# A spectral mixing kernel: the first chunk's input summed in PSUM, one row by cosines alone, and channel products spread one to a slot

## The chip, the cores and the metric

The kernel runs on one core of a Trainium2 chip. The metric is the device time of one execution in microseconds (us). The kernel before took 505.17 us, the median of three runs (504.72 to 506.06).

## The reference

For x of shape (8, 3136, 256), so 8 batches of 3136 rows:

```
X  = real part of fft(fft(x, axis=1), axis=2)
h  = X^T U V                       # U: 3136x32, V: 32x3136, along the rows
u  = X + h^T
out = u + max(u @ w1, 0) @ w2      # w1: 256x1024, w2: 1024x256
```

Everything is float32 outside; the kernel computes its products in bf16 with float32 sums.

## The kernel before, in words

**The transform along the rows** is a product with tables of sines (`tabs[0]`) and cosines (`tabs[1]`, shown as tabc). Symmetry is used four times. The rows n and 3136-n are folded (`along_d`, L255, and `alone`, L265, fold along d; `mirror`, L278, and `half`, L282, along n), on VectorE from two float32 copies of a batch in SBUF (xf by an indirect DMA on GpSimd's queue, L53; xr by a DMA of SyncE's queue, L70; each has a fringe of one partition, loaded by `load_0`, L76 and L79). The folded batch is `G[b % 2][par]`, bf16: columns 0 to 127 go with the sines, 128 to 255 with the cosines, 256 and 257 belong to d = 128. The tables carry 32 further columns (393 to 424), the table times U, so that one product gives the transform and its projection on U; for d = 128 another 32 columns (425 to 456), written by `u_128` (L541). So a product is QW = 425 or TW = 457 columns wide.

**seq(b, par, typ, pn)** (L303) makes one product group: four or eight matmuls (L327) into a PSUM bank. typ 0 is the sine part, typ 1 the cosine part; par and pn are the parities of the output and of the fold. The group pn = 0 is copied out by ScalarE (`ev`, L335), and when pn = 1 is there VectorE adds and subtracts the two into the rows of `B` (typ 0, L351 and L355) or `A` (typ 1, L351 and L353), and the U part into `tab` (L339). In typ 0, pn = 0, four of the eight matmuls put d = 128 into row 0 of B.

**The transform along d** works on column groups of 392 (`chan`, L366, and `chan_odd`, L374): A times a cosine matrix, copied by ScalarE to `ca` (L372), B times a sine matrix, then VectorE writes S = ca + psb and T = ca - psb (L381, L382). `lowrank` (L385) makes `TA` from `tab` (copied by ScalarE, L394). What symmetry leaves apart is put into further rows of `VA`, whose first 32 rows are V: the odd half of one column by `apart_odd` (L410, a DMA and a ScalarE copy L416) and d = 128 by `apart_128` (L396, three ScalarE copies L402, L404, L406 and a DMA L408).

**front(c)** (L431) makes `u` for a chunk of 512 rows, channels on partitions: TA times VA in PSUM (`ph`, L437), then VectorE adds S or T (L445), then a transposing DMA of SyncE's queue gives `ut`. **first_product** (L451): 16 matmuls with W1 (L457) per chunk in eight slots, each slot's result through a Relu on ScalarE into `h` (L459). **second_product** (L461): 32 matmuls with W2 (L473) per chunk, VectorE adds `ut` (L479 to L482), a DMA stores the chunk. There are 49 chunks of eight slots.

**The order.** Up to slot 22 the program is in the order written (`manual_schedule`, closed at L663); behind it a scheduler moves the instructions of each engine. Each engine, and each DMA queue, takes its instructions in order. The steps of later batches are put into the slots by `spread` (L648): for batch b the fold (`fold`, L286) from slot end-49 to mid, the transform (`transform`, L492) from mid to end, where end is the slot in which front(c + 1) first needs batch b (slot 43 for batch 1) and mid = end-19 (end-21 for batch 1). Inside a transform `chan(ch)` and `chan_odd(ch)` follow each other.

Batch 0 has no earlier chunk beside it: tables, fold, products, lowrank, channel groups 0 and 1, then front(0) and the first W1 product come one after another. There the products of the sine part are begun (part 0) when half of G is there, and the group's cosine matmuls for d = 128 come later (part 1), when columns 128 to 257 are folded. PSUM has three banks with the tag "dft" (products, channel groups, ph), three with "p1" (W1's results, and three of the first products), two for W2's.

Of the kernel before, what the change touches and what calls it, by code (L numbers as in the profile page):

```python
# [28 lines left out]
def kernel(  # L29
# [101 lines left out]
    EOR_ = cpool.tile([KP, 2, NI, 258], BF16, name="eor")  # L131
    EOS = cpool.tile([KP, 2, NI, 258], BF16, name="eos")
    for t in (EOF_, EOR_):
        nc.vector.memset(t.rearrange("p a i d -> p (a i) d")[:, :, 0:1], 0.0)
        nc.vector.memset(t.rearrange("p a i d -> p (a i) d")[:, :, 256:258], 0.0)
    G = [[cpool.tile([KP, NI, GW], BF16, name=f"g{s}{par}", tag=f"g{s}{par}") for par in range(2)]
         for s in range(2)]
    for par in range(2):
# [123 lines left out]
            nc.vector.tensor_tensor(dst[:, a, :, 192:256], src[:, a, :, 1:128:2],  # L262
                                    src[:, a, :, 255:128:-2], op=AL.add)

    def alone(a, src, dst):  # L265
# [20 lines left out]
    def fold(b):  # L286

        nxt = b + 1 < B
        for a in range(2):
            for src, dst, load in ((xr, EOR_, load_r), (xf, EOF_, load_f)):  # L290
                yield lambda a=a, src=src, dst=dst: (alone(a, src, dst), along_d(a, src, dst, 0))
                yield lambda a=a, src=src, dst=dst: along_d(a, src, dst, 1)
                if nxt:
                    yield lambda a=a, load=load: load(b + 1, a)
            yield lambda a=a: mirror(a, slice(0, 128), AL.subtract)
            yield lambda a=a: mirror(a, slice(128, 258), AL.add)
        if nxt:
            yield lambda: load_0(x, xf, xr, b + 1, D)
        for par in range(2):
            yield lambda par=par: half(b, par, slice(0, 128))  # L300
            yield lambda par=par: half(b, par, slice(128, 258))

    def seq(b, par, typ, pn, part=None):  # L303
# [11 lines left out]
        if part == 1 or (part == 0 and ("pt", par, pn) in d):  # L315
            pt = d["pt", par, pn]
        elif part == 0 and (par, pn) != (0, 1):
            pt = psum.tile([P, TW], FP32, tag="p1", name="pt1", bufs=3)
        else:
            pt = psum.tile([P, TW], FP32, tag="dft", name="pt", bufs=3)  # L320
        mm = [(typ, 128 * typ, i) for i in ktiles(pn)]
        if typ == 0 and pn == 0:
            mm += [(1, 256, i) for i in ktiles(0)]
        for n, (t, col, i) in enumerate(mm):
            if part is None or (part == 1) == (col == 256):
                w = TW if typ == 0 and (pn == 1 or n == 0 or col == 256) else QW
                nc.tensor.matmul(pt[:, :w], g[:kp(i), i, col:col + P], tabs[t][:kp(i), i, par, :w],  # L327
                                 start=(n == 0), stop=(n == len(mm) - 1))
        w = QW if typ == 1 else TW
        if part == 0:  # L330
            d["pt", par, pn] = pt
            return
        if pn == 0:
            ev = d["ev", par] = wp.tile([P, TW], FP32, tag="ev", name="ev", bufs=2)
            nc.scalar.copy(ev[:, :w], pt[:, :w])  # L335
# [4 lines left out]
        if typ == 0:  # L340
# [24 lines left out]
    def chan(b, ch):  # L365

        d = ST[b]
        lo, hi = columns(ch)
        pt = d["pst"] = psum.tile([P, NQ], FP32, tag="dft", name="pst", bufs=3)
        nc.tensor.matmul(pt[:, :hi - lo], MC1[:], d["A"][:, lo:hi], start=True, stop=True)  # L370
        ca = d["ca"] = wp.tile([P, NQ], FP32, tag="ca", name="ca", bufs=2)
        nc.scalar.copy(ca[:, :hi - lo], pt[:, :hi - lo])  # L372

    def chan_odd(b, ch):  # L374

        d = ST[b]
        lo, hi = columns(ch)
        pt = psum.tile([P, NQ], FP32, tag="dft", name="psb", bufs=3)
        nc.tensor.matmul(pt[:, :hi - lo], MS1[:], d["B"][:, lo:hi], start=True, stop=True)  # L379
        ca = d["ca"]  # L380
        nc.vector.tensor_tensor(d["S"][:, lo:hi], ca[:, :hi - lo], pt[:, :hi - lo], op=AL.add)  # L381
        nc.vector.tensor_tensor(d["T"][:, lo:hi], ca[:, :hi - lo], pt[:, :hi - lo],  # L382
                                op=AL.subtract)
# [9 lines left out]
                n += 1  # L393
        nc.scalar.copy(TA[b % 2][:R, :], pt[:])  # L394

    def apart_128(b, part, lo=0, hi=HALF // 2 + 1):  # L396


        Q = HALF // 2
        row, v = VA[b % 2][R:R + 1], ST[b]["B"][0:1]  # L400
        if part == 0:
            nc.scalar.copy(row[:, lo:hi], v[:, Q - lo:(Q - hi if hi <= Q else None):-1])  # L402
# [89 lines left out]
    def transform(b):  # L492

        for par, typ in ((0, 1), (0, 0), (1, 1), (1, 0)):
            for pn in range(2):
                yield lambda par=par, typ=typ, pn=pn: seq(b, par, typ, pn)
        yield lambda: (lowrank(b), apart_odd(b, 0), apart_128(b, 3))
        yield lambda: apart_128(b, 0)
        yield lambda: apart_odd(b, 1)
        for ch in range(4):  # L500
            yield lambda ch=ch: chan(b, ch)
            yield lambda ch=ch: chan_odd(b, ch)
            if ch in (1, 2):
                yield lambda ch=ch: apart_128(b, ch)

    CK = {}
    ST = {}
# [24 lines left out]

    for part in range(2):
        along_d(0, xr, EOR_, part)
    alone(0, xr, EOR_)
    for part in range(2):
        along_d(1, xr, EOR_, part)
    alone(1, xr, EOR_)
    us, uc = list(transform_u(0)), list(transform_u(1))

    def u_128(pk):  # L541
# [15 lines left out]

    for a in range(2):
        along_d(a, xf, EOF_, 0)
        alone(a, xf, EOF_)  # L560
        mirror(a, slice(0, 128), AL.subtract)
    u_128(1)
    for par in (1, 0):
        half(0, par, slice(0, 128))

    nc.gpsimd.iota(pint[:], pattern=[[0, 1]], base=D, channel_multiplier=-1)
# [10 lines left out]
        load_r(1, a)  # L577
    halve(1)

    for par in (1, 0):  # L580
        for pn in range(2):
            seq(0, par, 0, pn, 0)
        if par == 1:
            uc[2]()
            uc[3]()
            u_128(0)
    for a in range(2):
        along_d(a, xf, EOF_, 1)
        mirror(a, slice(128, 258), AL.add)
# [51 lines left out]
    front(0)
    for ch in range(2, 4):
        chan(0, ch)
        chan_odd(0, ch)
# [58 lines left out]
```

## Time and profile before

| what | value |
|---|---|
| median of three runs | 505.17 us |
| the profiled execution | 506.69 us, span 504.9 us, mean granted clock 0.988 |
| TensorE busy | 466.4 us (92%), 3024 matmuls |
| VectorE busy | 340.3 us (67%) |
| ScalarE busy | 302.9 us (60%) |
| GpSimd busy | 57.6 us (11%) |
| DMA | 68.68 MB, mean 136 GB/s |
| W1, W2 matmuls (L457, L473) | 212.4 and 204.1 us |
| product groups (L327) | 78.3 us, 320 matmuls |
| TensorE busy in 0 to 30, 30 to 52, 52 to 60 us | 11.40, 16.96, 6.61 us |
| TensorE busy in 60 to 70, 70 to 80, 80 to 90 us | 9.27, 10.00, 7.25 us |
| VectorE busy in 60 to 70, 70 to 80, 80 to 90 us | 10.00, 8.27, 9.97 us |
| TensorE busy in 100 to 150, 200 to 250, 400 to 450 us | 49.16, 49.50, 47.97 us |

Times are from the start of the span. The views are: the chain that ended last (each piece was released by the one above it), the waits (who waited for whom, in total, times, longest), the timeline of an engine, and the busy time in stretches. In a timeline the first two numbers are start and duration, and the bracket is the idle time before the first instruction of the row with what released it. In a table of stretches the number behind the POOL column is the clock that was granted to TensorE.

### The profile page before, as it was taken

What the parts mean: (1) busy time and instruction counts of PE and PEld (TensorE: products, weight loads), DVE (VectorE), ACT (ScalarE), POOL (GpSimd) and SP (SyncE); (2) the same over time, 40 slices, a digit from 0 to 9 for tenths busy, and PEclk for the clock granted to TensorE, in tenths of its full rate; (3) what the DMA queues carried; (4) which work ended last, traced back from release to release, by engine and by line L of the source; (5) the groups of instructions that cost most, each with busy time, mean ns of one, the idle gap of its engine ahead of it and who ended that gap; (6) DMA issues with size and microseconds to landing.
All of it is one profiled execution on the core that took longest, in us unless ns stands there. A gap on an engine that the chain in (4) does not pass through costs nothing.

```text
span 504.9 us, 8167 instructions
## 1 busy us (share of the span) xinstructions
PE 466.4 (92%) x3024; PEld 294.6 (58%) x3024; DVE 340.3 (67%) x825; ACT 302.9 (60%) x541; POOL 57.6 (11%) x124
## 2 busy tenths in 40 slices
PE   0777797999999999999999999999999999899997
PEld 0643364556655666566656665566656665566665
DVE  8848998989799989999386246653545335444343
ACT  6915763575648654765567654955576555855662
POOL 6137034101122021120000000000000000000000
PEclk9999898999999999999999999999999999999999
DMA  6695497949977596585422533234233343333433
GB/s 185 172 197 138 109 227 162 233 116 235 214 203 205 161 265 182 134 209 136 108 69 75 126 83 80 64 105 126 64 78 84 106 124 55 86 84 106 125 84 125
DMA packets 84371, 68.68 MB, mean 136 GB/s; under 512 B 53854, under 2 KB 80292, under 8 KB 81180
## 3 DMA queue, kind: packets, MB, share of 16 engines
q1 hardware_dynamic: 80764, 53.41, 41.6%
q0 software_dynamic: 3568, 14.76, 10.7%
q8 instruction: 23, 0.38, 0.3%
q14 instruction: 16, 0.13, 0.1%
HBM read 29.26 MB, written 25.69 MB: 109 GB/s over the span
## 4 chain that ended last, share of the span: by engine, by line
PE 75%; ACT 9%; DVE 7%; DMA 5%; issue 2%; POOL 0%; SPq 0%; DVEq 0%; ACTq 0%; POOLq 0%
PE p L473 29%; PE p L457 28%; PE pt L327 10%; PE ph L437 4%; ACT h L459 3%; PE pu L223 2%; DMA uf<-in_moe_U_dram,xidx 2%; ACT va L416 1%; DMA xr<-in_x_dram 1%; DMA va<-A 1%; ACT ca L372 1%; ACT va L404 1%; PE psb L379 1%; DVE u L445 1%; ACT va L402 1%
## 5 line engine op out<-in xcount | busy, mean ns | idle before, releaser
L459 ACT ACTIVATE h<-p 128x512 bf16<-128x512 f32 x392 | 217.9, 597 | 127.1 <-PE p L457 126.5
L457 PE MATMUL p<-u,w 128*128 128x512 bf16 x784 | 212.4, 382 | 1.6 <-ACT h L459 1.6
L473 PE MATMUL p<-w,h 128*128 128x256 bf16 x1568 | 204.1, 273 | 0.4 <-ACT h L459 0.4
L473 PEld LDWEIGHTS <-h 128*128 128x128 bf16 x1568 | 153.5, 98 | 62.0 <-issue 2.6
L457 PEld LDWEIGHTS <-w 128*128 128x128 bf16 x784 | 76.3, 98 | 70.3 <-issue 13.8
L479 DVE TENSOR_TENSOR o<-p,ut 128x4 f32<-128x4 f32 (+1 forms) x100 | 16.0, 160 | 100.7 <-PE p L473 97.5
L327 PEld LDWEIGHTS <-g 98*128 98x128 bf16 x320 | 32.8, 104 | 41.7 <-issue 10.1
L327 PE MATMUL pt<-tabc,g 98*128 98x425 bf16 (+1 forms) x192 | 46.2, 377 | 6.0 <-DVE g L283 3.3
L335 ACT COPY ev<-pt 128x457 f32<-128x457 f32 (+1 forms) x32 | 16.9, 527 | 43.8 <-PE pt L327 41.3
L482 DVE TENSOR_TENSOR o<-p,ut 128x254 f32<-128x254 f32 (+1 forms) x100 | 40.5, 405 | 0.0
L481 DVE TENSOR_TENSOR o<-p,ut 128x254 f32<-128x254 f32 (+1 forms) x100 | 40.5, 405 | 0.0
L445 DVE TENSOR_TENSOR u<-ph,S 128x512 bf16<-128x512 f32 (+15 forms) x64 | 35.0, 556 | 1.0 <-PE ph L437 1.0
L327 PE MATMUL pt<-tabs,g 98*128 98x457 bf16 (+2 forms) x128 | 32.1, 380 | 3.5 <-DVE g L283 3.5
L437 PE MATMUL ph<-va,ta 128*128 128x512 bf16 (+18 forms) x128 | 31.6, 332 | 4.0 <-DVE T L382 1.9
L445 DVE TENSOR_TENSOR u<-ph,T 128x512 bf16<-128x512 f32 (+15 forms) x64 | 34.9, 555 | 0.0
L381 DVE TENSOR_TENSOR S<-ca,psb 128x392 bf16<-128x392 f32 (+1 forms) x32 | 18.0, 562 | 21.0 <-ACT ca L372 16.0
L53 POOL DMA_INDIRECT xf<-in_x_dram,xidx x16 | 19.2, 1203 | 110.6 <-DVE eof L262 68.8
L283 DVE TENSOR_TENSOR g<-eos 99x1024 bf16<-99x1024 bf16 (+1 forms) x32 | 21.4, 689 | 6.4 <-PE pt L327 6.4
L279 DVE TENSOR_TENSOR eos<-eof,eor 99x1024 bf16<-99x1024 bf16 (+1 forms) x32 | 21.0, 687 | 0.8 <-POOL eof L274 0.7
L257 DVE TENSOR_TENSOR eor<-xr 99x1016 bf16<-99x1016 f32 x16 | 19.3, 1208 | 1.5 <-DMA xr<-in_x_dram 1.5
L223 PE MATMUL pu<-gu,tabs 98*98 98x32 bf16 (+1 forms) x64 | 6.0, 251 | 15.1 <-DVE gu L194 15.1
L257 DVE TENSOR_TENSOR eof<-xf 99x1016 bf16<-99x1016 f32 x16 | 19.3, 1206 | 0.3 <-POOL eof L274 0.3
(113 smaller groups left out, 313.3 us busy)
## 6 DMA issues: line engine op xcount, KB each, us to landing
out_dram<-o SPq DMA_DIRECT2D x48, 512.0 KB
xr<-in_x_dram SPq DMA_DIRECT2D x16, 784.0 KB
va<-A SPq DMA_DIRECT2D x7, 196.1 KB
ut<-u SPq DMA_TRANSPOSE x49
w<-in_moe_w_ch_dram POOLq DMA_DIRECT2D x1, 512.0 KB, 10.6
out_dram<-o SPq DMA_DIRECT2D x4, 128.0 KB
va<-in_moe_V_dram POOLq DMA_DIRECT2D x2, 196.0 KB, 8.6
xf<-in_x_dram,xidx POOLq DMA_INDIRECT x16, 7.9
```

The source lines that it names most:

```text
L53: nc.gpsimd.indirect_dma_start(out_, None, bass.AP(t.tensor, t.offset, [[w, rows], [1, w]]), bass.IndirectOffsetOnAxis(idx, 0), element_of ...
L257: nc.vector.tensor_tensor(dst[:, a, :, 1:128], src[:, a, :, 1:128], src[:, a, :, 255:128:-1], op=AL.subtract)
L279: nc.vector.tensor_tensor(EOS[:, a, :, cols], EOF_[:, a, :, cols], EOR_[:, a, ::-1][:, :, cols], op=op)
L283: nc.vector.tensor_tensor(G[b % 2][par][:, :, cols], EOS[:, 0, :, cols], EOS[:, 1, :, cols], op=AL.add if par == 0 else AL.subtract)
L327: nc.tensor.matmul(pt[:, :w], g[:kp(i), i, col:col + P], tabs[t][:kp(i), i, par, :w], start=(n == 0), stop=(n == len(mm) - 1))
L437: nc.tensor.matmul(ph[:, col:col + hi - lo], TA[b % 2][:, s * P:(s + 1) * P], VA[b % 2][:, lo:hi], start=True, stop=True)
L445: nc.vector.tensor_tensor(u[:, s, col:col + hi - lo], ph[:, col:col + hi - lo], src, op=AL.add)
L457: nc.tensor.matmul(p1[:], W1[:, s, j * P:(j + 1) * P], k["u"][:, s, :], start=(s == 0), stop=(s == 1))
L459: nc.scalar.activation(k["h"][:, j, :], p1[:], AF.Relu)
L473: nc.tensor.matmul(p2[:, t % w, :], h[:, j, rs], W2[:, j, :], start=(j == 0), stop=(j == JT - 1))
L481: nc.vector.tensor_tensor(o[:, ts, 1:P], p2[:, :w, 1:P], ut[:, ts, 1:P], op=AL.add)
L482: nc.vector.tensor_tensor(o[:, ts, P + 1:D], p2[:, :w, P + 1:D], ut[:, tT, P - 1:0:-1], op=AL.add)
```

## The change

Three things, all written out in the program.

**Batch 0's d = 128.** `alone(0, ...)` puts columns 0 and 128 of x side by side with one GpSimd copy instead of a copy and a signed product, and `seq` takes the column that goes to row 0 of B through the cosine table for both parities: four matmuls more in the groups (typ 0, pn = 1), none wider than 425. So `u_128` is not needed before batch 0's products; it goes to slots 8 and 10. Row 0 of B holds the finished row, so VA gets it by one DMA and one ScalarE copy (slot 12) in place of four ScalarE copies, a DMA and a VectorE operation. Parity 0 is taken first.

**The first chunk.** A new `front_first` sums u in two PSUM banks: sine matrix times B, cosine matrix times A, TA times V's 32 rows; ScalarE copies one half to `u`, VectorE the other. The channel groups of batch 0 are no longer ahead of it: chan(0, 0) follows it, and the slots 0 to 3 take chan(0, ch + 1) and chan_odd(0, ch).

**Later batches.** In `transform`, chan_odd(ch - 1) follows chan(ch), the ScalarE copy of `apart_odd` comes behind chan(0) instead of ahead of it, and the 21 steps are spread from mid to end-3. The fold of batch 1 starts at slot 4 instead of 2.

```diff
+    def alone(b, a, src, dst):
+        if b == 0:
+            nc.gpsimd.tensor_copy(dst[:, a, :, 128:257:128], src[:, a, :, 0:129:128])
+            return
...
         mm = [(typ, 128 * typ, i) for i in ktiles(pn)]
-        if typ == 0 and pn == 0:
+        if typ == 0 and b == 0:
+            mm += [(1, 256, i) for i in ktiles(1 - pn)]
+        elif typ == 0 and pn == 0:
             mm += [(1, 256, i) for i in ktiles(0)]
+        tw = TW if typ == 0 and b > 0 else QW
...
+        if b == 0:
+            if part == 0:
+                nc.sync.dma_start(out=row[:, :HALF + 1], in_=v)
+            elif part == 2:
+                nc.scalar.copy(row[:, HALF + 1:], v[:, HALF - 1:0:-1])
...
-        yield lambda: apart_odd(b, 1)
         for ch in range(4):
             yield lambda ch=ch: chan(b, ch)
-            yield lambda ch=ch: chan_odd(b, ch)
-            if ch in (1, 2):
-                yield lambda ch=ch: apart_128(b, ch)
+            yield (lambda: apart_odd(b, 1)) if ch == 0 else (lambda ch=ch: chan_odd(b, ch - 1))
+            if ch > 1:
+                yield lambda ch=ch: apart_128(b, ch - 1)
+        yield lambda: chan_odd(b, 3)
...
-    u_128(1)
-    for par in (1, 0):
+    for par in range(2):
         half(0, par, slice(0, 128))
...
-            u_128(0)
...
-    apart_128(0, 3)
-    lowrank(0)
-    nc.scalar.copy(VA[0][P // 2:, :CH], ST[0]["A"][P // 2:, :CH])
-    apart_odd(0, 0, CH)
-    for ch in range(2):
-        chan(0, ch)
-        chan_odd(0, ch)
...
+    def front_first():
+        u = cp.tile([P, 2, CH], BF16, tag="u", name="u", bufs=2)
+        ph = [psum.tile([P, CH], FP32, tag="p1", name="ph1", bufs=3) for s in range(2)]
+        h = [slice(s * P, (s + 1) * P) for s in range(2)]
+        for s in range(2):
+            nc.tensor.matmul(ph[s][:], MSN[:, h[s]], ST[0]["B"][:, :CH], start=True, stop=False)
+        lowrank(0)
+        for s in range(2):
+            nc.tensor.matmul(ph[s][:], MC[:, h[s]], ST[0]["A"][:, :CH], start=False, stop=False)
+        for s in range(2):
+            nc.tensor.matmul(ph[s][:], TA[0][:R, h[s]], VA[0][:R, :CH], start=False, stop=True)
+        nc.scalar.copy(u[:, 0], ph[0][:])
+        nc.vector.tensor_copy(u[:, 1], ph[1][:])
+        ut = cp.tile([P, 2 * CH // P, P], BF16, tag="ut", name="ut", bufs=3)
+        nc.sync.dma_start_transpose(out=ut[:], in_=u.rearrange("p s r -> p (s r)"))
+        CK[0] = dict(u=u, ut=ut)
+    front_first()
+    apart_odd(0, 0)
+    chan(0, 0)
...
+    for ch in range(4):
+        due[ch] = [lambda ch=ch: chan_odd(0, ch)]
+        if ch < 3:
+            due[ch].insert(0, lambda ch=ch: chan(0, ch + 1))
+    spread([lambda: apart_odd(0, 1), lambda: u_128(0), lambda: u_128(1), lambda: apart_128(0, 2)],
+           6, 14)
...
-        spread(list(fold(b)), max(end - 49, 2), mid)
-        spread(steps, mid, end)
+        spread(list(fold(b)), max(end - 49, 4), mid)
+        spread(steps, mid, end - 3)
```

More of the change, by code (lines that the diff above doesn't have):

```diff
@@ L133 @@
     for t in (EOF_, EOR_):
-        nc.vector.memset(t.rearrange("p a i d -> p (a i) d")[:, :, 0:1], 0.0)
-        nc.vector.memset(t.rearrange("p a i d -> p (a i) d")[:, :, 256:258], 0.0)
+        nc.vector.memset(t.rearrange("p a i d -> p (a i) d")[:, :, 0:258:257], 0.0)
     G = [[cpool.tile([KP, NI, GW], BF16, name=f"g{s}{par}", tag=f"g{s}{par}") for par in range(2)]
@@ L263, in along_d @@
                                     src[:, a, :, 255:128:-2], op=AL.add)
-    def alone(a, src, dst):
+    def alone(b, a, src, dst):
+        if b == 0:
+            nc.gpsimd.tensor_copy(dst[:, a, :, 128:257:128], src[:, a, :, 0:129:128])
+            return
         nc.gpsimd.tensor_copy(dst[:, a, :, 128:129], src[:, a, :, 0:1])
@@ L290, in fold @@
             for src, dst, load in ((xr, EOR_, load_r), (xf, EOF_, load_f)):
-                yield lambda a=a, src=src, dst=dst: (alone(a, src, dst), along_d(a, src, dst, 0))
+                yield lambda a=a, src=src, dst=dst: (alone(b, a, src, dst), along_d(a, src, dst, 0))
                 yield lambda a=a, src=src, dst=dst: along_d(a, src, dst, 1)
@@ L314, in seq @@
         g = G[b % 2][par]
-        if part == 1 or (part == 0 and ("pt", par, pn) in d):
-            pt = d["pt", par, pn]
+        if part == 1:
+            pt = d.pop(("pt", par, pn))
         elif part == 0 and (par, pn) != (0, 1):
@@ L321, in seq @@
         mm = [(typ, 128 * typ, i) for i in ktiles(pn)]
-        if typ == 0 and pn == 0:
+        if typ == 0 and b == 0:
+            mm += [(1, 256, i) for i in ktiles(1 - pn)]
+        elif typ == 0 and pn == 0:
             mm += [(1, 256, i) for i in ktiles(0)]
+        tw = TW if typ == 0 and b > 0 else QW
         for n, (t, col, i) in enumerate(mm):
             if part is None or (part == 1) == (col == 256):
-                w = TW if typ == 0 and (pn == 1 or n == 0 or col == 256) else QW
+                w = tw if pn == 1 or n == 0 or col == 256 else QW
                 nc.tensor.matmul(pt[:, :w], g[:kp(i), i, col:col + P], tabs[t][:kp(i), i, par, :w],
                                  start=(n == 0), stop=(n == len(mm) - 1))
-        w = QW if typ == 1 else TW
         if part == 0:
@@ L334, in seq @@
             ev = d["ev", par] = wp.tile([P, TW], FP32, tag="ev", name="ev", bufs=2)
-            nc.scalar.copy(ev[:, :w], pt[:, :w])
+            nc.scalar.copy(ev[:, :tw], pt[:, :tw])
             return
@@ L339, in seq @@
         nc.vector.tensor_tensor(d["tab"][:, typ, par, :], pt[:, NQ:QW], ev[:, NQ:QW], op=AL.add)
-        if typ == 0:
+        if tw > QW:
             nc.vector.tensor_tensor(d["tab"][0:1, 0, par, :], pt[0:1, QW:TW], ev[0:1, QW:TW],
@@ L368, in chan @@
         lo, hi = columns(ch)
-        pt = d["pst"] = psum.tile([P, NQ], FP32, tag="dft", name="pst", bufs=3)
+        pt = psum.tile([P, NQ], FP32, tag="dft", name="pst", bufs=3)
         nc.tensor.matmul(pt[:, :hi - lo], MC1[:], d["A"][:, lo:hi], start=True, stop=True)
-        ca = d["ca"] = wp.tile([P, NQ], FP32, tag="ca", name="ca", bufs=2)
+        ca = d["ca", ch] = wp.tile([P, NQ], FP32, tag="ca", name="ca", bufs=2)
         nc.scalar.copy(ca[:, :hi - lo], pt[:, :hi - lo])
@@ L379, in chan_odd @@
         nc.tensor.matmul(pt[:, :hi - lo], MS1[:], d["B"][:, lo:hi], start=True, stop=True)
-        ca = d["ca"]
+        ca = d.pop(("ca", ch))
         nc.vector.tensor_tensor(d["S"][:, lo:hi], ca[:, :hi - lo], pt[:, :hi - lo], op=AL.add)
@@ L394, in lowrank, with apart_128 @@
         nc.scalar.copy(TA[b % 2][:R, :], pt[:])
-    def apart_128(b, part, lo=0, hi=HALF // 2 + 1):
+    def apart_128(b, part):
         Q = HALF // 2
         row, v = VA[b % 2][R:R + 1], ST[b]["B"][0:1]
-        if part == 0:
-            nc.scalar.copy(row[:, lo:hi], v[:, Q - lo:(Q - hi if hi <= Q else None):-1])
+        if b == 0:
[3 more added lines that the diff above has]
+                nc.scalar.copy(row[:, HALF + 1:], v[:, HALF - 1:0:-1])
+        elif part == 0:
+            nc.scalar.copy(row[:, :Q + 1], v[:, Q::-1])
         elif part == 1:
@@ L534 @@
         along_d(0, xr, EOR_, part)
-    alone(0, xr, EOR_)
+    alone(0, 0, xr, EOR_)
     for part in range(2):
         along_d(1, xr, EOR_, part)
-    alone(1, xr, EOR_)
+    alone(0, 1, xr, EOR_)
     us, uc = list(transform_u(0)), list(transform_u(1))
@@ L559 @@
         along_d(a, xf, EOF_, 0)
-        alone(a, xf, EOF_)
+        alone(0, a, xf, EOF_)
         mirror(a, slice(0, 128), AL.subtract)
-    u_128(1)
-    for par in (1, 0):
+    for par in range(2):
         half(0, par, slice(0, 128))
@@ L578 @@
     halve(1)
-    for par in (1, 0):
+    for par in range(2):
         for pn in range(2):
             seq(0, par, 0, pn, 0)
-        if par == 1:
+        if par == 0:
             uc[2]()
             uc[3]()
-            u_128(0)
     for a in range(2):
@@ L600 @@
         phase(pd[t][:], lrow.rearrange("p a l -> p (a l)"), pcol[:, t:t + 1], 17)
-    seq(0, 1, 0, 0, 1)
+    for pn in range(2):
+        seq(0, 0, 0, pn, 1)
     sine(MSN[:, 0:128], pd[0][:, 0:128], 17, -1)
     sine(MSN[:, 128:256], pd[0][:, 128:256], 17, 1)
-    seq(0, 0, 0, 0, 1)
+    seq(0, 1, 0, 0, 1)
     cosine(MC[:], pd[1][:], 17)
@@ L608 @@
     nc.scalar.copy(MC1[:], MC[:, :P])
+    seq(0, 1, 0, 1, 1)
     nc.gpsimd.tensor_copy(gate[0:1, 2:3], G[0][1][0:1, 0, 128:129])
@@ L624 @@
         nc.gpsimd.memset(G[1][par][:, :, 258:GW].bitcast(I32), 0)
-    for par in (1, 0):
-        seq(0, par, 0, 1, 1)
+    apart_128(0, 0)
     for par in range(2):
@@ L629 @@
             seq(0, par, 1, pn)
-            if (par, pn) == (0, 0):
-                apart_128(0, 0, 0, CH)
-    apart_128(0, 3)
-    lowrank(0)
-    nc.scalar.copy(VA[0][P // 2:, :CH], ST[0]["A"][P // 2:, :CH])
-    apart_odd(0, 0, CH)
-    for ch in range(2):
-        chan(0, ch)
-        chan_odd(0, ch)
     setup.close()
     cp = ctx.enter_context(tc.tile_pool(name="cp", bufs=2))
[L641 to L644, printed above, removed]
+    def front_first():
[17 more added lines that the diff above has]
+    chan(0, 0)
     due = {}
@@ L650, in spread @@
             due.setdefault(lo + (hi - lo) * n // len(steps), []).append(step)
-    spread([lambda: apart_128(0, 0, CH), lambda: apart_128(0, 1)], 1, 3)
-    spread([lambda: apart_odd(0, 1), lambda: apart_128(0, 2)], 7, 13)
+    for ch in range(4):
[4 more added lines that the diff above has]
+           6, 14)
     for b in range(1, B):
```

## The prediction

> **What bounds the kernel now.** I read the page first: TensorE is busy 92% of the span, so a change can win only where TensorE is idle or slow. The table of stretches says where: 11.4 of the first 30 us, 17.0 of the next 22, 7.25 of 10 at 80 to 90, and 49.2 of 50 from 100 on. So I read the chain of work that ended last, from 20 to 55 us:
>
> ```profile
> 26.38 0.29 DVE tabs L544
> 26.67 0.20 DVE tabc L544
> 26.87 0.61 DVE g L283
> 27.49 0.05 issue
> 27.54 3.15 PE pt L327 x8
> 30.69 2.87 PE pu L223 x32
> ...
> 34.02 0.29 DVE tabs L544
> 34.32 0.20 DVE tabc L544
> 34.52 0.59 DVE eof L260
> ...
> 38.41 1.32 DVE g L283 x2
> 39.74 0.05 issue
> 39.78 7.72 PE pt L327 x24
> 47.51 0.65 PE ptt L391 x4
> ```
>
> The reader is to see that `u_128` (L544) stands on the chain twice, and that the fold (L260 to L283) stands behind it only because VectorE takes its queue in order. The waits say what VectorE idled for in front of it:
>
> ```profile
> DVE tabs L544 <- ACT tabc L228: 5.6, 1, 5.6
> ...
> DVE tabs L544 <- ACT tabc L247: 1.7, 1, 1.7
> ```
>
> From the last product (47.50) to the first W1 matmul (53.29) there are 5.8 us of lowrank, channel groups and S, T, u with TensorE mostly waiting.
>
> The third place is batch 1. VectorE's timeline:
>
> ```profile
> 78.98 1.22 DVE L257 TENSOR_TENSOR eor<-xr 99x1016 bf16<-99x1016 f32 x1 [1.46 <-DMA xr<-in_x_dram]
> ```
>
> That is the fold of batch 2, placed by the scheduler ahead of batch 1's sums (L351, L353, done at 84.4), which free the bank that TensorE waits for (2.75 us, until 84.55). And the clock:
>
> ```profile
> 52.00:53.00 1.00, 0.70 (x3) 0.19 (x2) 1.00 (x3) 0.48 (x1) 0.00 (x0) 0.98 0.00 0
> 53.00:54.00 1.00, 1.00 (x4) 0.41 (x3) 1.00 (x3) 0.48 (x1) 0.00 (x0) 0.50 0.02 8
> 56.00:57.00 1.00, 0.71 (x3) 0.15 (x2) 1.00 (x2) 0.98 (x3) 0.00 (x0) 0.81 0.00 0
> ```
>
> The granted clock is half from 53.0 to 56.4, and again from 83.7 to 90.5. Ahead of 46.0 the column shows 1.00, but the matmuls themselves show otherwise: 425 columns go every 0.355 us, behind 46.0 every 0.18. So batch 0's products run at half clock until then. The changes of speed, 46.1, 53.0, 56.4, 83.7 and 90.5, lie on one grid of 3.41 us: full speed comes at a grid point after a step that was nearly all matmuls (87% busy was not enough at 42.7), half speed after one that was about half busy; 68% kept it.
>
> **The change part by part.**
>
> *Up to the fold.* GpSimd's products with signs go for batch 0, and with them two waits of 0.34 us (VectorE, L279); `u_128`'s wait of 1.7 us and its 0.5 us go. VectorE ends L279 at 23.96 (was 24.64), half of parity 0 at 24.6 (was 27.48), parity 1 at 25.2, L235 at 25.6. Then nothing holds it: two times 0.6 + 0.6 + 0.7, then g 2 x 0.65. The second half is there at 30.7 instead of 39.72, 9 us earlier. The batch 1 loads that follow (xf, GpSimd's queue) meet those of W1, V and W2, which are ahead of them in that queue and about 2 us earlier; they landed 7 to 11 us after issue, so by 37; needed at 42.
>
> *Products.* From 24.65: 8 of 425 columns at 0.355 (2.8), the 32 small ones as before (3.1), 8 more (2.8): 33.4. Then 16 for d = 128 (before 8: the change adds 8) and 16 of typ 1, with no gap. The small ones do not raise the clock (64 of them in 15.05 to 21.0 kept 0.093 us each), so the first full grid step after 30.55 ends between 34.0 and 37.4; on the old grid at 35.9. Until then 7 of the 32 at 0.355, the others at 0.18: 40.5 (39.4 to 41.1; 44.8 if it never came) against 47.50.
>
> The 8 added matmuls are 1.4 us of that. ScalarE's chain beside it (ev 0.5, sines 0.7, ev 0.5, 0.5, 0.5, two copies 0.5) ends at 39.0, GpSimd's row of signs in the sine matrix at 39.6, its W1 cast (1.03, which u's memory waits for) at 40.7: just hidden, and GpSimd's queue holds nothing else that is due.
>
> *First u.* B's matmuls 2 x 0.22 (41.05), lowrank's four 0.45 (tab is ready at 40.9), A's two behind VectorE's first sum (41.4): 42.0; TA's copy 0.36 lies under them, TA's two end at 42.45, and their result is read 0.17 later. A copy of 128x512 from PSUM on VectorE is not in the trace: L445's add of that size 0.68, L459 on ScalarE 0.60, bounds 0.5 and 0.7; I take 0.6, beside ScalarE's. First W1 matmul at 43.3 against 53.29: **10 us earlier**, 5.6 if the clock stayed at half.
>
> *What then is late.* All four channel groups now lie behind u. ScalarE is paced by ca 0.44 + h 0.52 a slot, VectorE by S and T, 0.94 a slot: they end at 48.1. The next u waits for the DMA of A into VA, which in SyncE's queue stands behind the transpose (1.3 us): issued at 45.2, with 2.74 to 4.27 us (the two rows of it on the chain, 367.72 and 422.80) landed at 47.9 to 49.4. I take the lower end, since the DMA engines moved nothing at 46 to 50 before. u of chunk 1 is done at 49.7 to 51.1, 6.4 to 7.8 us behind the first W1 (before 6.2). Copies L402 and L404 (1.3 us of ScalarE in that path) go. The B row's DMA (one partition; no row times its landing) has 9 us of cover, and the late copy of 1567 columns costs at most L416's 1.49 on ScalarE, which at 67 to 73 idles 0.6 to 1.1 us ahead of each pair of Relus.
>
> VectorE did batch 1's first L257 to L262 (2.33) in the gap ahead of that u; now they come behind it, with u_128's four (1.0). Before, u's end to the last g took 59.5 to 76.0, 16.5; now 19.8: 69.5 to 70.9, a gain of 5.1 to 6.5. So **of the 10 us about 4 are given back**: the first W1 is no longer what sets the end, VectorE's queue is. Batch 2's loads follow its folds, so the DMA that ended at 78.95 moves by about 5.3, and batch 1's first sums stand 1.34 us (L262 and the three of L479 to L482) further ahead in the new order: done at 84.4 - 5.3 - 1.34 = 77.8. TensorE goes on 6.7 us earlier than at 84.55.
>
> *Later batches.* From 100 on TensorE waits 2.0 us in all for `ca` ahead of psb, 1.6 for T ahead of ph, 1.1 for ca ahead of ph and pst. The first goes, since psb now comes a slot behind its ca. Bounds: all 4.7 gained, or lost in the rival below. I take 2.0.
>
> **Sum.** 504.9 - 6.7 - 2.0 = 496.2 of span. The profiled run took 506.69 and the median is 505.17; taken off the median: **496.5 us**.
>
> **The rivals.**
>
> *A: no half clock after batch 1's wait.* TensorE will again wait 2 to 3 us there; before, that cost 83.7 to 90.5 at half speed, of which 84.55 to 90.5 is 3.0 us of work. If the wait falls across a grid point, neither step is half idle and the 3.0 are saved, as far as VectorE (9.97 of 10 busy there) follows: 493.5 us. For it: 68% busy kept the clock at 59.8. Against: the wait is of the same size as before. [...]
>
> *B: the transfer is hidden anyway.* The DMA engines are full at 70 to 80 (share 1.01). If batch 2's xr still lands at 78.95, the sums come only the 1.34 earlier: 505.2 - 1.3 - 2.0 = 501.9. Against: the engines are near idle at 46 to 54, and the loads are issued by the folds.
>
> *C: the clock stays at half in batch 0.* First W1 at 47.7, slots of 1.5 us by TensorE (0.86 + 0.33 + 0.33), u of chunk 1 at 56.1, last g at 75.9: only the 1.3 stays, and 503.9 if later batches give nothing. It needs a gap in the products, such as a late g.
>
> *D: slower.* The eight groups of a transform go in 16 x 8/21 = 6 slots instead of 7, and the new order sets more of them side by side. A group's bank (three of "dft") is free only when VectorE has done three operations (0.17, 0.57, 0.59), and VectorE is 45.4 of 50 busy at 100 to 150 with folds up to 1.2 us long. Four waits of 1.2 in each of batches 1 to 3 are 14.4: 505.2 - 6.7 + 14.4 = 512.9. It decides from 0.7 us a wait. Against: the waits at that place are nil in the trace of batch 2 and later, and the new order keeps 1.3 us or more of other matmuls ahead of most.
>
> That the first u isn't summed as said is no rival: the changed kernel's instruction order shows the six matmuls and one add less on VectorE.
>
> **How the numbers follow.** Forecast 0.48, A 0.15, B 0.15, C 0.10, D 0.12. About 0.3% (1.5 us) is what a measurement of this kernel can tell from no change. Forecast, A and B are faster: 0.78; C is the same: 0.10; D slower: 0.12. The range leaves D out and reaches to C (504), and below A by half of the 4.7 us of waits: 491.5.
>
> **What would show it.** The second g at 31 (not 39.7); 425-column products every 0.18 us from about 36; first W1 at 43 to 44; chunk 1's u 6 to 8 us behind it; VectorE without idle time from there to the last g at 70; products of batch 1 waiting for g, which they did not before; TensorE's wait for A ending near 78; the waits for ca ahead of psb gone. It is wrong if VectorE's long stretch is not what batch 1 waits for (then up to 10 us stay), or if waits for A, B or g appear in batches 2 to 7.

## The result, and the profile after

The changed kernel took **498.63 us**, the median of four runs (497.33 to 500.51), against 505.13 us for the kernel before (504.72 to 506.06): a ratio of 0.987, 95% interval 0.984 to 0.991. It is faster, by 6.5 us (1.3%). The forecast was 496.5 us, in a range of 491.5 to 504.0.

The profiled execution took 498.67 us, span 496.9, against 506.69 and 504.9: 8.0 us less, where the sum had 8.7. VectorE is busy for 340.1 us, ScalarE for 299.4. TensorE's 461.2 us can't be held against the 466.4 before: 56 of its 3036 matmuls left no record in this profile. A second profile, which has them all, says 465.8.

This is the same view as the first one before, the chain of the work that ended last; columns are start, duration, what:

```profile
23.68 0.70 DVE g L285
24.39 0.05 issue
24.43 3.02 PE pt L332 x8
27.46 2.86 PE pu L222 x32
30.32 10.40 PE pt L332 x40
...
42.66 0.59 ACT u L653
43.26 0.04 issue
43.30 0.72 PE p L466 x2
...
45.06 3.21 DMA va<-A
48.27 0.14 issue
48.41 0.59 PE ph L446 x2
49.00 0.45 PE p L466 x2
49.44 0.67 DVE u L454
50.11 1.12 DVE eor L256
```

The reader is to see that `u_128` and the folds no longer stand among the products, that these go in one piece to 40.72, and that from the DMA of A into VA the chain goes to VectorE, and from u straight into batch 1's fold. Lines are shifted: products L332, W1 L466, front L446 and L454, folds L256 to L285, A L357.

The table of stretches has the clock behind the POOL column:

```profile
36.00:37.00 1.00, 1.00 (x5) 0.46 (x4) 0.90 (x3) 0.00 (x0) 0.00 (x0) 1.00 1.30 246
37.00:38.00 1.00, 1.00 (x7) 0.52 (x6) 0.35 (x2) 0.87 (x2) 0.00 (x0) 1.00 1.36 256
...
77.00:78.00 1.00, 0.36 (x2) 0.19 (x3) 1.00 (x5) 0.00 (x0) 0.00 (x0) 0.80 0.32 82
78.00:79.00 1.00, 1.00 (x4) 0.40 (x3) 1.00 (x3) 0.00 (x0) 0.00 (x0) 0.50 0.77 287
...
81.00:82.00 1.00, 1.00 (x8) 0.64 (x7) 0.97 (x5) 0.21 (x1) 0.00 (x0) 0.99 1.14 362
```

Four or five matmuls a us become seven at about 36.5, where the forecast had 35.9: batch 0's products did reach full clock. Behind batch 1's wait the clock is half for one step of 3.4 us (77.6 to 81.0); before it was two (83.7 to 90.5). That holds for this execution only: in the second profile of the changed kernel the matmuls go at half speed from the end of that wait, 78.64, to about 83.6 (four of 425 columns in 1.58 us, 0.9 at full speed), which is more than one step, and 12 W1 matmuls from 49.21 took 4.44 us where the first profile has 2.85. That wait, and VectorE's work ahead of it, in the timelines of TensorE and VectorE:

```profile
77.64 1.58 PE L332 MATMUL pt<-tabc,g 98*128 98x425 bf16 x4 [3.33 <-DVE A L357]
```

```profile
73.41 1.22 DVE L256 TENSOR_TENSOR eor<-xr 99x1016 bf16<-99x1016 f32 x1 [1.18 <-DMA xr<-in_x_dram]
...
76.92 0.58 DVE L357 TENSOR_TENSOR A<-ev,pt 128x392 bf16<-128x392 f32 x1
```

In TensorE's timeline before, the same wait was

```profile
84.55 1.58 PE L327 MATMUL pt<-tabc,g 98*128 98x425 bf16 x4 [2.75 <-DVE A L353]
```

The pattern is the old one, 6.9 us earlier: batch 2's fold waits for its DMA, batch 1's sums stand behind it, TensorE behind them. The DMA was issued at 65.39 and took 7.92 us; before, at 71.67 and 7.28.

From 100 us on TensorE's waits were 6.0 us in all, of these

```profile
PE psb L379 <- ACT ca L372: 2.0, 5, 0.5
PE ph L437 <- DVE T L382: 1.6, 4, 0.5
...
PE ph L437 <- ACT ca L372: 0.6, 2, 0.4
```

and are 3.6, of these

```profile
PE ph L446 <- ACT ca L376: 2.0, 4, 0.8
PE p L482 <- ACT h L468: 1.1, 2, 0.7
...
PE psb L383 <- ACT ca L376: 0.2, 1, 0.2
```

(us in total, times, longest). The 2.0 for `ca` ahead of psb is now 0.2 and the 1.6 for T is gone; the wait for `ca` ahead of ph rose from 0.6 to 2.0.

**Where the 10 us went** is read best from the starts of the transposes of ut, one a chunk, in the timeline of SyncE's queue, each less that of before (us). The rows below the first are the experiments, each one profiled execution.

| kernel | chunk 0 | 1 | 2 | 4 | 6 | 8 | 48 |
|---|---|---|---|---|---|---|---|
| after | -9.45 | -9.39 | -6.27 | -5.58 | -7.12 | -7.13 | -8.02 |
| after, again | -9.84 | -9.02 | -5.90 | -4.58 | -5.80 | -5.81 | -7.54 |
| old transform | -10.16 | -8.38 | -5.25 | -4.54 | -4.39 | -4.39 | -3.66 |
| new transform alone | 0.76 | 0.85 | 0.84 | -0.72 | -1.76 | -1.77 | -3.46 |
| groups first | -6.02 | -6.96 | -3.84 | -2.28 | -3.85 | -3.86 | -5.79 |
| fold in the gap | -7.40 | -7.58 | -6.76 | -8.69 | -9.56 | -9.57 | -11.10 |
| fold 2 behind | -10.42 | -10.22 | -7.10 | -13.67 | -13.51 | -7.68 | -11.30 |
| A's DMA ahead | -11.34 | -11.41 | -8.29 | -9.86 | -10.12 | -10.12 | -11.35 |
| these three | -8.38 | -8.77 | -7.95 | -14.53 | -14.37 | -9.20 | -11.62 |
| fold in two gaps | -10.61 | -11.00 | -9.07 | -8.42 | -10.00 | -10.01 | -12.17 |
| and u_128 on GpSimd | -10.02 | -10.41 | -8.88 | -8.46 | -7.74 | -7.74 | -9.94 |

In the changed kernel 3.1 us are lost from chunk 1 to chunk 2, on VectorE, another 0.7 by chunk 4, and 2.4 come back later. In its second profile, the same kernel stands up to 1.3 us from the first, so smaller differences between two rows say nothing.

### The profile page after: what moved, and what is told of

The parts are those of the page before. It is cut to its first block, busy times and chain, and to the rows that moved or that the text cites. A ratio compares the mean times of both kernels' runs of the same rounds, so it can differ in the third digit from the quotient of the medians.

```text
span 496.9 us, 8110 instructions
## 1 busy us (share of the span) xinstructions
PE 461.2 (93%) x2980; PEld 293.4 (59%) x3036; DVE 340.1 (68%) x819; ACT 299.4 (60%) x538; POOL 63.8 (13%) x120
## 4 chain that ended last, share of the span: by engine, by line
PE 66%; DVE 14%; DMA 8%; ACT 8%; issue 3%; POOL 0%; SPq 0%; DVEq 0%; ACTq 0%; POOLq 0%
PE p L482 26%; PE p L466 25%; PE pt L332 9%; PE ph L446 4%; ACT h L468 3%; DMA va<-A 3%; DMA out_dram<-o 2%; DVE eof L256 2%; DVE eor L256 2%; DMA uf<-in_moe_U_dram,xidx 2%; DMA xr<-in_x_dram 2%; ACT va L425 1%; DVE u L454 1%; ACT ca L376 1%; DVE eor L261 1%
## 5 line engine op out<-in xcount | busy, mean ns | idle before, releaser
L466 PE MATMUL p<-u,w 128*128 128x512 bf16 x729 | 202.7, 380 | 4.4 <-DVE u L454 1.5
L466 PEld LDWEIGHTS <-w 128*128 128x128 bf16 x784 | 75.9, 98 | 69.5 <-issue 9.2
L332 PEld LDWEIGHTS <-g 98*128 98x128 bf16 x328 | 32.9, 103 | 35.4 <-issue 7.0
L332 PE MATMUL pt<-tabc,g 98*128 98x425 bf16 (+1 forms) x200 | 44.9, 366 | 3.6 <-DVE A L357 3.3
L339 ACT COPY ev<-pt 128x425 f32<-128x425 f32 (+1 forms) x32 | 16.8, 526 | 40.2 <-PE pt L332 32.1
L490 DVE TENSOR_TENSOR o<-p,ut 128x254 f32<-128x254 f32 (+1 forms) x100 | 40.5, 405 | 0.0
L53 POOL DMA_INDIRECT xf<-in_x_dram,xidx x16 | 22.9, 1431 | 100.7 <-DVE eof L261 43.7
L454 DVE TENSOR_TENSOR u<-ph,S 128x512 bf16<-128x512 f32 (+23 forms) x63 | 34.2, 553 | 0.4 <-PE ph L446 0.4
L454 DVE TENSOR_TENSOR u<-ph,T 128x512 bf16<-128x512 f32 (+23 forms) x63 | 34.1, 552 | 0.0
L446 PE MATMUL ph<-va,ta 128*128 128x512 bf16 (+15 forms) x126 | 29.8, 328 | 4.4 <-ACT ca L376 2.0
L332 PE MATMUL pt<-tabs,g 98*128 98x457 bf16 (+2 forms) x128 | 31.8, 378 | 1.0 <-DVE g L285 0.9
L285 DVE TENSOR_TENSOR g<-eos 99x1024 bf16<-99x1024 bf16 (+1 forms) x32 | 21.3, 688 | 4.5 <-PE pt L332 4.4
L343 DVE TENSOR_TENSOR tab<-pt,ev 128x32 bf16<-128x32 f32 x32 | 6.0, 187 | 22.6 <-PE pt L332 22.2
L256 DVE TENSOR_TENSOR eof<-xf 99x1016 bf16<-99x1016 f32 x16 | 19.3, 1207 | 1.3 <-POOL eof L276 1.3
L256 DVE TENSOR_TENSOR eor<-xr 99x1016 bf16<-99x1016 f32 x16 | 19.3, 1206 | 1.2 <-DMA xr<-in_x_dram 1.2
```

Of the source, the lines that this page charges most:

```text
L53: nc.gpsimd.indirect_dma_start(out_, None, bass.AP(t.tensor, t.offset, [[w, rows], [1, w]]), bass.IndirectOffsetOnAxis(idx, 0), element_of ...
L256: nc.vector.tensor_tensor(dst[:, a, :, 1:128], src[:, a, :, 1:128], src[:, a, :, 255:128:-1], op=AL.subtract)
L285: nc.vector.tensor_tensor(G[b % 2][par][:, :, cols], EOS[:, 0, :, cols], EOS[:, 1, :, cols], op=AL.add if par == 0 else AL.subtract)
L446: nc.tensor.matmul(ph[:, col:col + hi - lo], TA[b % 2][:, s * P:(s + 1) * P], VA[b % 2][:, lo:hi], start=True, stop=True)
L454: nc.vector.tensor_tensor(u[:, s, col:col + hi - lo], ph[:, col:col + hi - lo], src, op=AL.add)
L466: nc.tensor.matmul(p1[:], W1[:, s, j * P:(j + 1) * P], k["u"][:, s, :], start=(s == 0), stop=(s == 1))
```

## The experiments

The theory: two parts make the gain, the front (VectorE's queue from the first u to the last g sets what is left of it) and the new transform of later batches. The rivals: the front alone, or a gain that is hidden behind batch 2's DMA. A diff is against the changed kernel unless said otherwise.

**The parts one by one.** These four ran beside each other; the kernel before took 505.18 us there (23 runs, 503.18 to 507.04).

Old transform, with the new front:

```diff
+        yield lambda: apart_odd(b, 1)
         for ch in range(4):
             yield lambda ch=ch: chan(b, ch)
-            yield (lambda: apart_odd(b, 1)) if ch == 0 else (lambda ch=ch: chan_odd(b, ch - 1))
...
+            yield lambda ch=ch: chan_odd(b, ch)
...
-        spread(steps, mid, end - 3)
+        spread(steps, mid, end)
```

> The changed kernel with the old transform: chan_odd(ch) right behind chan(ch), apart_odd's copy ahead of chan(0), steps spread to end. Theory: the sums of batch 1 stand 1.34 us later again on VectorE (L262 and the three additions to o ahead of them), and the waits for ca ahead of psb come back (1.7 us from chunk 4 to the last): 498.6 + 3.0 = 501.6 us, 0.993 of before. Rival (the later batches' part is worth nothing): 498.6 us, 0.987.

Measured: 503.01 us (12 runs, 499.41 to 506.64), ratio 0.995 (0.992 to 0.997). The median is 1.4 us above the theory's 501.6, which the interval (501.3 to 503.7 us) still holds; the rival's 498.6 lies outside. TensorE's waits for psb and for T from 100 us on are again those of before:

```profile
PE psb L383 <- ACT ca L376: 2.0, 5, 0.5
PE ph L446 <- DVE T L386: 1.9, 5, 0.5
```

New transform alone, on the kernel before:

```diff
-        spread(steps, mid, end)
+        spread(steps, mid, end - 3)
```

and the new order of its steps, as in the change.

> The kernel before with only the new transform (chan_odd a step later, apart_odd's copy behind chan(0), steps spread to end-3). Theory: the two gains of the part stand by themselves: 1.34 us at batch 1's wait for A (83.2 instead of 84.55) and 1.7 us later on: 502.1 us, 0.994 of before. Rival (denser transforms wait more for their PSUM banks, and the start hides it): 505 us or slower.

Measured: 502.57 us (6 runs, 501.18 to 504.4), ratio 0.994 (0.992 to 0.996), near the theory's 502.1 and against the rival. In TensorE's timeline the wait that was 2.75 us, until 84.55, is

```profile
82.51 0.89 PE L327 MATMUL pt<-tabc,g 98*128 98x425 bf16 x4 [0.29 <-DVE A L353]
```

and 1.8 us for A ahead of ph come behind it.

So each part is worth about half: 0.53% and 0.59%, together 1.1%, against 1.28% for the change. Whoever would have put the whole gain down to the first chunk, where 10 us are to be seen, would have missed half of it.

The changed kernel once more, as a control:

> The changed kernel again, beside the three others on the same chip: 498.6 us, 0.987 of before; wait for A ending at 77.6 us. If the start of its span differs from the first profile it will be in when TensorE's full speed comes in batch 0's products (34 to 37.4 us), since that grid is not tied to the program.

Measured: 499.23 us (6 runs, 496.03 to 502.37), ratio 0.988 (0.984 to 0.991). The time repeats, the places do not: batch 1's wait for A took 3.95 us and ended at 78.64, 1.0 later than in the first profile, although the first W1 matmul came 0.4 earlier, at 42.90.

Channel groups 0 and 1 ahead of the first u, as before the change, and the old front(0):

```diff
+    lowrank(0)
+    nc.scalar.copy(VA[0][P // 2:, :CH], ST[0]["A"][P // 2:, :CH])
+    apart_odd(0, 0, CH)
+    for ch in range(2):
+        chan(0, ch)
+        chan_odd(0, ch)
...
-    front_first()
-    apart_odd(0, 0)
-    chan(0, 0)
+    front(0)
```

> The changed kernel with channel groups 0 and 1, the copies into VA and the old front(0) put back ahead of the first W1 product; d = 128 by cosines alone and the new transform stay. Theory (VectorE's queue, from the first chunk's S and T to batch 1's first sums, sets the end of the start): the first W1 product starts 3 us later (40.6 + 5.8 = 46.4 against 43.3), chunk 1's u 2.5 us later, and all of that reaches the end, since VectorE has no idle time behind it: batch 1's wait for A ends near 80 (77.6 in the changed kernel) and the time is 501.1 us, 0.992 of before. Rival (the PSUM sum is hidden anyway, the gain came from the fold alone): 498.6 us and A at 77.6.

Measured: 502.11 us (10 runs, 498.12 to 505.42), ratio 0.993 (0.990 to 0.995). The number fits the theory (the wait for A ended at 80.94, where it had "near 80"), but its reason is mixed: the first W1 matmul came at 47.55 and not at 46.4. In TensorE's timeline:

```profile
44.97 1.01 PE L446 MATMUL ph<-va,ta 128*128 128x512 bf16 x2 [3.32 <-DMA va<-B]
```

The DMA of one row of B, 3.1 KB, was issued at 37.5 and landed 7.3 us later; in the changed kernel the DMA engines' share is 0.81 to 1.36 from 37 to 42 us. So this run does not price the order of the groups by itself; it shows what the cover that the prediction gave this DMA (9 us) is worth. It also has d = 128 by cosines and the new transform, and its ratio is 0.993 where the new transform alone has 0.994: what the new d = 128 is worth without the new first u can't be told from nothing.

**Where the 3 us behind chunk 1 go.** Four kernels ran beside each other, and two more later; the kernel before took 504.95 us there (10 runs) and 504.57 us (11 runs).

Batch 1's first fold (2.33 us) in VectorE's gap behind `phase`:

```diff
+    alone(1, 0, xr, EOR_)
+    for part in range(2):
+        along_d(0, xr, EOR_, part)
```

and it leaves `fold`.

> The changed kernel with the first piece of batch 1's fold (L256, L259, L261 and the GpSimd part, 2.33 us of VectorE) moved from behind chunk 1's u to the 2.6 us in which VectorE waits for batch 0's first product (33.5 to 36.1). No work changes. Theory (VectorE's queue from chunk 1's u on sets when batch 1's sums are done): the whole queue moves up by 2.3 us, batch 1's wait for A ends near 75.3 instead of 77.6 and the time is 496.6 us, 2.3 under the changed kernel. Rival (batch 2's fringe of xr, which takes 7.9 us to land with the DMA engines near full, is what VectorE waits for anyway): A at 77 or later, 498.9 us.

Measured: 496.38 us (4 runs, 495.83 to 499.11), ratio 0.985 (0.982 to 0.988). The time is the theory's; the way there is not. VectorE's timeline and TensorE's:

```profile
35.97 1.22 DVE L256 TENSOR_TENSOR eor<-xr 99x1016 bf16<-99x1016 f32 x1 [4.33 <-DMA xr<-in_x_dram]
```

```profile
39.52 2.52 PE L333 MATMUL pt<-tabc,g 98*128 98x425 bf16 x8 [2.13 <-DVE B L360]
```

The gap was not free: batch 1's data came only at 35.97, the fold held batch 0's sums up, the products waited 2.13 us for a bank, and the first W1 matmul came at 45.35, 2 us later than in the changed kernel. Still chunk 2 lost 0.8 instead of 3.1, and batch 1's wait for A fell from 3.33 to 0.7 us (with 1.8 for A ahead of ph behind it, where the changed kernel has 0.5). Late at the front, early where it counts.

Batch 2's fold behind batch 1's sums:

```diff
-            if 8 * c + j == 22:
+            if 8 * c + j == 44:
                 order.close()
```

> The changed kernel with the written order kept up to slot 44 instead of 22, so that batch 2's fold stands behind all of batch 1's sums on VectorE instead of ahead of the first. Theory: TensorE's wait for A (3.3 us) goes, and with it the stretch at half clock behind it (77.8 to 81.0, 1.6 us of work): 494 us. Rival (that fold is only put off: VectorE is busy 97 in 100 from 84 to 100, and batch 2's products then wait for g): what is gained at 78 is given back by 150, 498.9 us or more.

Measured: 497.97 us (4 runs, 495.38 to 499.25), ratio 0.987 (0.984 to 0.989). The wait for A and the half clock behind it are gone, and chunk 4 stands at -13.67. By chunk 8 six of these are given back: batch 2's fold now comes late, and VectorE's queue holds up the output. TensorE's waits at 70 to 115 us:

```profile
PE p L466 <- DVE u L454: 1.7, 2, 1.5
PE p L482 <- DVE o L491: 1.3, 1, 1.3
```

The time lies between the theory's 494 and the rival's 498.9. The rival's direction came true and its wait did not: TensorE waited for u and o, not for g. VectorE's order moved the wait. Why this execution is at -11.30 again by chunk 48 stays open.

A's DMA ahead of the first transpose:

```diff
     def front_first():
...
         nc.vector.tensor_copy(u[:, 1], ph[1][:])
+        apart_odd(0, 0)
...
     front_first()
-    apart_odd(0, 0)
```

> The changed kernel with the DMA of A into VA issued ahead of the first transpose in SyncE's queue, as soon as A is there (42 instead of 45). Theory: chunk 1's u then waits for S and T alone, and VectorE's queue moves by its idle time ahead of that u, 0.35 us in the first profile and 1.1 in the second: 498.2 us, with less spread between runs, since that DMA takes 3.2 us in one profile and 3.4 or 4.7 in others. Rival (TensorE's wait ahead of that u is what counts): 1.4 to 2.1 us.

Measured: 496.97 us (5 runs, 495.33 to 497.79), ratio 0.984 (0.982 to 0.986). From chunk 0 to chunk 1 it took 6.36 us; the changed kernel 6.49, and 7.25 in its second profile. So 0.1 to 0.9 us can be the edit's there. The theory's step failed: issued at 40.12 instead of 45.06, the DMA took 6.14 us instead of 3.21, and TensorE still waited 1.24 us for it (1.36 in the changed kernel, 2.13 in its second profile). Of the 2.0 us by which chunk 1 is ahead of the changed kernel's, 0.6 are an earlier start of the products and 1.3 the clock: they took less time although nothing among them was changed (32 in 7.77 there):

```profile
32.31 6.51 PE L332 MATMUL pt<-tabc,g 98*128 98x425 bf16 x32
```

The median is 1.7 and 2.3 us under the changed kernel's two. That is nearer the rival's number than the theory's 498.2, but the rival's reason, that wait, fell by 0.1 or 0.9 us only; what gave the rest is open.

The three together:

> The three before together: the fold's first piece in the gap, the DMA into VA ahead of the transpose, the written order up to slot 44. Theory: the effects lie in one chain and add up, less what the next bound takes: 2.3 + 0.7 + 4.9 under the changed kernel would be 491; with TensorE busy nearly all the way from chunk 1 on, no more than its waits between 47 and 88 us (9.6 us in the first profile) can go. Rival (put-off folds come back as waits for g in batch 2): 496 us or more.

Measured: 495.59 us (4 runs, 495.05 to 500.01), ratio 0.984 (0.980 to 0.988). Again 14.5 us at chunk 4 and 9.2 at chunk 8, with the same waits for u and o (1.7 and 1.3): the gains do not add.

The fold in places that are idle and have the data, with A's DMA ahead:

```diff
+        along_d(0, xr, EOR_, 2)
         nc.scalar.copy(u[:, 0], ph[0][:])
         nc.vector.tensor_copy(u[:, 1], ph[1][:])
+        along_d(0, xr, EOR_, 3)
```

where parts 2 and 3 are the two additions of part 1, which leave `fold`.

> A's DMA ahead of the first transpose, as in the run with that edit alone, and two additions of batch 1's first fold (0.68 us each) taken from the stretch behind chunk 1's u into VectorE's two idle places of 0.9 and 0.87 us on either side of its copy of the first u, where their data have landed. Theory (VectorE's queue behind the first u is what gives back a third of the gain): last g 1.3 us earlier, the loss between chunk 1 and chunk 2 falls from 3.1 us to about 1.8, wait for A ends 1.3 us earlier by the first W1 matmul's time, 495.7 us or ratio 0.9815. Rival 1 (VectorE is full again in 90 to 110 us whatever comes before, as the run with three edits had it): the transposes' gain at chunk 8 stays at 10.1 us or less and the time is 497. Rival 2 (as in the run where the whole fold was put into the earlier gap, the moved work delays the products or the first u): first W1 0.3 to 2 us later, 497 to 498.

Measured: 496.42 us (5 runs, 494.5 to 497.75), ratio 0.984 (0.981 to 0.987). The step itself did what the theory said: chunk 2 lost 1.9 us, not 3.1. But batch 2's fold then waited for its data (the first line's GpSimd had itself waited for the fringe of xf until 67.74), in VectorE's timeline:

```profile
68.15 1.22 DVE L256 TENSOR_TENSOR eof<-xf 99x1016 bf16<-99x1016 f32 x1 [1.20 <-POOL eof L277]
70.56 1.22 DVE L256 TENSOR_TENSOR eor<-xr 99x1016 bf16<-99x1016 f32 x1 [1.18 <-DMA xr<-in_x_dram]
```

With A's DMA alone ahead, the second of these ran at 69.15 with no wait. So 1.3 us of VectorE's work taken out of 48 to 67 us became a wait for a transfer at 67 to 71, and neither 495.7 nor 497 can be told from what was measured. From the first W1 matmul to the end of the wait for A it took 32.65 us, and 31.96 with A's DMA alone ahead: the theory's 1.3 us did not get that far. In this execution the mechanism of the prediction's rival B bounds the next step: the fringe of xr was issued 0.8 us earlier than with A's DMA alone (62.60 against 63.39) and landed later (VectorE waited for it until 70.56; with A's DMA alone it had it by 69.15).

And u_128 on GpSimd:

```diff
-            nc.vector.tensor_tensor(
+            nc.gpsimd.tensor_tensor(
                 tabs[t][:, t::2, pk, QW:TW], tabs[1][:, t::2, pk, NQ:QW],
```

> The same, and u_128's four products (0.2 to 0.29 us each on VectorE, 1.0 in all) given to GpSimd, which is idle there. Theory: another 1.0 us off VectorE's full stretch, the loss between chunk 1 and chunk 2 near 0.8 us, 494.7 us or ratio 0.9795. Rival 1: no difference to the run beside it. Rival 3: GpSimd takes several us for the four, and batch 1's first products of the sine part wait for the table: PE waits ahead of pt in 60 to 70 us, 496 or more.

Measured: 496.37 us (6 runs, 494.63 to 497.37), ratio 0.983 (0.980 to 0.985): no difference to the run beside it, which is rival 1. Chunk 2 lost 1.5 us where 0.8 was said. GpSimd took 0.89 + 0.84 + 0.39 + 0.39 us for the four. A warning for readers of single profiles: by the spans (492.7 and 495.0) this kernel is 2.3 us slower than the one above, by the medians equal. The one profiled execution was the quickest of five, the other the slowest of six.

All these versions lie at 495.6 to 498.0; against the changed kernel's 498.6 and 499.2 the best are 2 to 3 us ahead. None of them ran beside that kernel, and with four to six runs each their intervals overlap one another's and its own.

## Why the prediction was right

- **The second half of g.** Forecast 30.7; it ended at 30.67.
- **Products and clock.** Forecast to end at 40.5, with full speed from 35.9; measured 40.72 and 36.5. Rival C did not come about.
- **The first u.** Forecast 43.3; the first W1 matmul came at 43.30. VectorE's copy of 128x512 from PSUM, which the trace of before does not have, took 0.69, near the upper bound of 0.7 and not the 0.6 taken. The first W1 matmul waited for ScalarE's half (0.59); VectorE's is needed by the second, and the pair took 0.71 where later ones take 0.59, so the difference cost 0.1 at most.
- **u of chunk 1.** Forecast for the DMA of A: 2.74 to 4.27 us, lower end taken; it took 3.21 and landed at 48.27. u was done at 50.1, inside 49.7 to 51.1. In other executions of the same transfer it took 3.44 and 4.73 us.
- **What is given back.** Forecast: the last g at 69.5 to 70.9, VectorE without idle time up to there. It ended at 69.75 and VectorE was busy throughout from 48.8. The runs with work taken out of this stretch confirm the cause of this loss: behind chunk 1 it fell from 3.1 to 1.9 when 1.36 us were taken out, and to 0.8 with 2.33.
- **Batch 1's wait.** Forecast 77.8; measured 77.64. That it is so close is in part luck. Its sum takes 5.3 us for the DMA of batch 2's xr, although the lower end that it says it takes for A's DMA gives 6.5 (76.0 - 69.5). The DMA was issued 6.3 us earlier, took 0.6 longer and landed 5.6 earlier, and the second profile has 78.64. From that DMA on, the order was worth 1.33 where 1.34 was said. Xr moved with its issue, which is against rival B. TensorE waited 3.33 us where "2 to 3 again" was said, and two small waits followed that no step had: 0.5 for A ahead of ph and 0.8 for u ahead of ptt. Together they are as long as the 1.3 us between the 6.9 and the gain of 5.6 at chunk 4.
- **Half clock.** The forecast kept it as it was; rival A let it vanish. In the profiled execution one of two steps went, in the second profile none, so no gain of the change can be booked on it. The gain rises from 5.6 at chunk 4 to 7.1 at chunk 6, but in the second profile, with both steps there, it rises by 1.2, and with the new transform alone by 1.0 (old transform: not at all). Where that rise comes from stays open. (The forecast's "87% busy" ahead of 42.7 is 85 by the trace: 2.90 of 3.41 us.)
- **Later batches.** Forecast 2.0; the waits fell by 2.4. A wait for B of 0.3 us appeared, which the forecast had named as a sign of being wrong; the second profile does not have it.
- **Front and transform.** The sum had 5.4 us for the front and 3.3 for the transform (1.3 of the wait for A came from the transform's order). By the medians of the runs that separate them, the transform is worth 2.6 us alone (505.18 - 502.57) and 3.8 on top of the front (503.01 - 499.23); the front is worth 2.2 alone (505.18 - 503.01) and 3.3 on top of the transform (502.57 - 499.23). So the front is the mis-sized term, at about half of its forecast. The spans of the single profiled executions give it more: 3.6 alone, and 501.5 - 496.9 = 4.6. With the old transform TensorE waited 4.25 us for A, until 80.01, 4.5 earlier than before, so of this gain, too, only a part reached the end.
- **Rival D.** From 100 us on no product (pt) is among TensorE's waits for VectorE; its longest wait there is 0.8 us, for ScalarE. A bank that comes late was not seen.

The sum was 0.7 us off in the span. The other 1.5 of the 2.1 us between 496.5 and 498.63 come from the last line of the sum: it took the gain off the median (505.17), worked from an execution that stood 1.5 us above it (506.69). The changed kernel's profiled execution stood on its median. So the span's close fit is luck in part: the two executions happen to differ by 8.0 us where the medians differ by 6.5, and by the medians the front falls short. Where the 1.5 us of the one execution come from isn't shown.

## What to carry to other kernels

When a start-up is shortened, ask which queue is next, and count what that queue still has to do: here the first result came 10 us earlier and 6 us reached the next batch, because VectorE's list between them had grown by 3.3. An idle place is worth filling only if its data have landed by then; the fold that was put into the largest gap waited 4.3 us for its data and held up the work behind it. And when the versions differ by 2 us and single executions by 4, read mechanisms from the traces and differences from medians.

## What the runs showed of the hardware

**The clock's steps come at other places in other executions.** The 32 products of batch 0 on the cosine table, started between 32.2 and 33.2 us and not changed, took 7.77 us in the changed kernel and 7.33 in its second profile, 7.50, 7.36, 6.95, 6.51 and 6.41 in five others. The count of matmuls a us goes from four to seven at 36.5 in the changed kernel and at about 33 in the one with A's DMA ahead. That moves the first W1 matmul by up to 1.4 us, as much as some of the versions above differ; the changed kernel's six later runs lie 6.3 us apart, 23 runs of before 3.9 (how much of that is the clock isn't shown). Behind batch 1's wait half speed ends at 81.0 in the first profile of the changed kernel and at about 83.6 in the second: 2.6 us apart, no whole step of 3.4, so the steps lie at other times of one and the same program.

**A wait shorter than a step can halve the clock.** In the run with A's DMA ahead, TensorE's timeline and the table of stretches have

```profile
80.58 0.39 PE L446 MATMUL ph<-va,ta 128*128 128x512 bf16 x1 [1.84 <-DVE A L357]
```

```profile
81.00:82.00 1.00, 1.00 (x4) 0.40 (x3) 1.00 (x2) 0.51 (x1) 0.00 (x0) 0.61 0.95 247
82.00:83.00 1.00, 0.98 (x3) 0.24 (x2) 1.00 (x3) 0.09 (x1) 0.00 (x0) 0.50 0.91 194
```

Half speed came from 81.2 to 84.6 behind a wait of 1.84 us; in the 3.42 us up to 81.2 TensorE was busy for 1.46, or 43%. Before, batch 1's wait ahead of the half clock was 2.75 us, in the changed kernel 3.33; this one is the shortest of the three. The length of the wait alone does not decide it. With the fold in the gap TensorE's timeline has the same wait, 1.2 us later, and the granted clock stayed at 1.00:

```profile
81.76 0.39 PE L447 MATMUL ph<-va,ta 128*128 128x512 bf16 x1 [1.84 <-DVE A L358]
```

```profile
82.00:83.00 1.00, 1.00 (x6) 0.48 (x5) 1.00 (x3) 0.38 (x1) 0.00 (x0) 1.00 0.87 259
```

What else decides it, no run here shows.

**A small DMA was not a short one.** One row of 3.1 KB, issued at 37.5 in the run with the groups first, took 7.3 us to land. A's 196 KB took 3.2 us in the changed kernel, where little else moved (share 0.11 in the us before), and 6.1 us in the run that issued it at 40.12, among other traffic (shares of 0.65 to 2.15 in the us from 40 to 45). What holds such a transfer up, the engines or its queue, no run separates.
